# First batch loaded and scaled by halves of its chunks, a weight piece loaded later

## The chip, the cores and the metric

The kernel runs on one core of one Trainium2 chip. The metric is the device time of one execution in microseconds (us). The inputs lie in DRAM, laid out in tiles; every DMA of the kernel is issued by one engine's queue, that of SyncE (SP).

## The reference, cut to what matters

A retention layer (attention with a decay in place of the softmax) is followed by two feed-forward stages. The change touches only how the first layer starts.

```python
# q, k, v: batch 4, heads 8, sequence 576, head size 64
scores = scale * np.matmul(q, k.transpose(0, 1, 3, 2))
ret = scores * Dmat[None]            # Dmat[h, i, j] = gamma[h] ** (i - j) for i >= j, else 0
x = np.matmul(ret, v)                # -> x: 2304 tokens x 512
a, b = x @ moe_w1, x @ moe_w2        # 512 x 1024 each, in float64 weights
x = (a * b @ moe_w3) @ moe_w_out     # then a second stage with moe2_w_in, moe2_alpha, moe2_w_out
```

## The kernel before, in words

The retention of a batch is cut into five chunks of 128 tokens (the last has 64) and into pairs of heads. For a chunk `c`, `scores(c)` multiplies keys by queries on TensorE (PE), VectorE (DVE) multiplies by the mask into `rt`, `moments(c)` makes the sum of key times value that later chunks need, and `values(c)` multiplies the state and `rt` by queries and values; the result is split into `xh` (ScalarE, ACT) and `xl` (DVE). The decay is put into the operands first: `scale` multiplies the queries on GpSimd (POOL), 512 columns (L396) and then 64 (L398) for each pair, and `prep` multiplies the keys on ACT (L389), two instructions of 256 columns for each pair.

Batch 0 is done as two groups, `r0` (pairs 0 and 1) and `r1` (pairs 2 and 3), in a list of steps written out at L602; `s0` and `s1` are their steps. Step `s0[0]` is scores(0) and moments(0), `s0[1]` is scores(1), values(0) and moments(1), and so on. `busy(n)` issues `n` matmuls on zeros (dummies), 26 before the first step and one behind each of the first four steps. `later` holds work for other engines, which `flush()` issues.

The weights of the next product, `w12`, are 16 pieces of 512 KB in float64 (here w0, w1, w2 and so on; `raw` in the trace). `Weights` takes a piece apart in four steps: `_first` is two ACT instructions (L93, L94), `_second` four on DVE (L103 to L108), `_third` one on ACT (L114, the upper part) and `_fourth` one on DVE (L122, the lower part). `tick` issues one such step for each of the four kinds where one is due, last kind first, after `load_until(at[0] + near)` has issued loads; `near` is 4. `tick(n)` begins no piece from number `n` on. `ws.until(n)` ticks until `n` pieces are done.

Behind batch 0 come the product units `ab_unit(0, c)` for c = 0, 1, 2 (L686 to L688), each two products of 12 matmuls (L188) with pieces 2c and 2c+1, with a step of the retention of batch 1 behind each of the two. In `ab_unit` the function `between` (L685) is called behind each product: it ticks the weights, flushes, and then ticks the retention of batch 1, whose first step is `prep` and `scale` of pairs 0 and 1. Before unit c, `ws.until(2c + 2)` stands.

PE, SP and ACT run their instructions in the order in which this program issues them; the order on DVE and POOL is chosen by a planner when the kernel is built.

The queue of SP before the change, in order: decay tables of rows (6 KB), tables of pairs 0 and 1 (448 KB), pairs 0 and 1 of batch 0 (576 KB of queries and keys and 544 KB of keys and values each), w0, tables of pairs 2 and 3, pairs 2 and 3, w1 to w3, pairs 2 and 3 of batch 1 (`load_apart`, 1120 KB each), w4 (by the second tick), pairs 0 and 1 of batch 1 (`loads`), w5 and on.

Of the kernel before, what the change touches and what calls it, by code (L numbers as in the profile page):

```python
# [7 lines left out]
F32 = mybir.dt.float32  # L8
# [3 lines left out]
AF = mybir.ActivationFunctionType  # L12
ALU = mybir.AluOpType
# [133 lines left out]
def retention_moe_kernel(ctx: ExitStack, tc, qk, kv, w_out1, w3t, w12, w_in, w_out2, alpha, c_row, c_pair, out):  # L147
    nc = tc.nc

    def pool(stack, name, bufs=1, **kw):  # L150
        return stack.enter_context(tc.tile_pool(name=name, bufs=bufs, **kw))
# [65 lines left out]
    ws = Weights(nc, raw_room, room, 4)  # L217
# [121 lines left out]
    attn = pool(pa, "attn", side="left")  # L339
# [4 lines left out]
    per_pair = decay.tile([P, NPAIR, 3 * CH + 64], F32, name="per_pair")  # L344
# [4 lines left out]
    kd, gc = per_row[:, 0:H], per_row[:, H:]  # L349
# [13 lines left out]
    def crossed(b):  # L363
        return b >= 2
# [6 lines left out]
    class Retention:  # L371
# [5 lines left out]
            self.ps = slice(pairs[0], pairs[-1] + 1)  # L377
            self.rt, self.state = {}, None

        def prep(self, pairs=None):  # L380
            for p in pairs or self.pairs:
                k = kvt[self.b][p]
                if self.b >= 3:
                    both = k[:, 0:8].rearrange("p (j c) d -> p j (c d)", j=2)
                    nc.gpsimd.tensor_tensor(out=both, in0=both, in1=kd[:, 2 * p:2 * p + 2].unsqueeze(2)
                                            .to_broadcast([P, 2, 4 * D]), op=ALU.mult)
                    continue
                for j in range(2):
                    nc.scalar.activation(k[:, 4 * j:4 * j + 4], k[:, 4 * j:4 * j + 4], AF.Copy,  # L389
                                         scale=kd[:, 2 * p + j:2 * p + j + 1])  # L390

        def scale(self, pairs=None):
            for p in pairs or self.pairs:
                q, by = qt[self.b][p], qs[:, p]
                full = q[:, 0:512].rearrange("p (c i) -> p c i", i=CH)
                nc.gpsimd.tensor_tensor(out=full, in0=full, in1=by.unsqueeze(1).to_broadcast([P, 4, CH]),  # L396
                                        op=ALU.mult)
                nc.gpsimd.tensor_tensor(out=q[:, 512:S], in0=q[:, 512:S], in1=by[:, 0:64], op=ALU.mult)  # L398

        def scores(self, c):  # L400
            b, n = self.b, self.n
# [107 lines left out]
    qt, kt, kvt, vt = ({b: {} for b in range(B)} for _ in range(4))  # L509

    def in_places(b, p, t, src):

        for rows, pp, _ in places(b, p):
            nc.sync.dma_start(out=t[rows], in_=src[pp])  # L514
# [10 lines left out]
    def load_pair(b, p):  # L525
        x = attn.tile([P, 2, S], F32, tag=f"qk{p}", name=f"qk{b}_{p}")
        y = attn.tile([P, 17, D], F32, tag=f"kv{p}", name=f"kv{b}_{p}")
        qt[b][p], kt[b][p], kvt[b][p], vt[b][p] = x[:, 0], x[:, 1], y[:, 0:16], y[:, 16]
        if crossed(b) and p % 2:
            in_places(b, p, x, qk[b, p])  # L530
            nc.sync.dma_start(out=y[:, 0:16], in_=kv[b, p, :, 0:16])
            in_places(b, p, y[:, 16], kv[b, p, :, 16])
        else:
            nc.sync.dma_start(out=x, in_=qk[b, p])
            nc.sync.dma_start(out=y, in_=kv[b, p])

    def load_apart(b, p, n):

        x, y, z = (in_wa(n + m, f"pair{b}_{p}_{m}").bitcast(F32).rearrange("p a b -> p (a b)") for m in range(3))
        qt[b][p], kt[b][p] = x[:, 0:S], y[:, 0:S]  # L540
        vt[b][p] = x[:, S:S + D]
        kvt[b][p] = z.rearrange("p (a d) -> p a d", d=D)
        nc.sync.dma_start(out=qt[b][p], in_=qk[b, p, :, 0])
        nc.sync.dma_start(out=kt[b][p], in_=qk[b, p, :, 1])
        nc.sync.dma_start(out=kvt[b][p], in_=kv[b, p, :, 0:16])
        nc.sync.dma_start(out=vt[b][p], in_=kv[b, p, :, 16])
# [11 lines left out]
    first = ExitStack()  # L558
    psum0 = attention_psum(first, 2)
    nc.sync.dma_start(out=per_row, in_=c_row)  # L560
    nc.sync.dma_start(out=per_pair[:, 0:2], in_=c_pair[:, 0:2])
    load_pair(0, 0)
    load_pair(0, 1)
    ws.load_until(1)
    nc.sync.dma_start(out=per_pair[:, 2:4], in_=c_pair[:, 2:4])
    load_pair(0, 2)
    load_pair(0, 3)
    ws.load_until(4)
    load_apart(1, 2, 10)
    load_apart(1, 3, 13)  # L570
    warm = pool(first, "ps_warm", space=PSUM).tile([P, 512], F32, name="warm")
# [1 line left out]
    def busy(n):  # L573
        for _ in range(n):
            nc.tensor.matmul(warm, idle[:, 0:P], idle[:, :512], start=True, stop=True)

    busy(26)
    r0, r1 = Retention(0, [0, 1], psum0), Retention(0, [2, 3], psum0)
    s0, s1 = r0.steps(), r1.steps()
    r0.scale()  # L580
    r0.prep()

    def keep_busy(step):
        def run():
# [4 lines left out]

    def ready(p):  # L590
        def run():
            r1.scale([p])
            r1.prep([p])
        return run

    def loads():
        load_pair(1, 0)
        load_pair(1, 1)

    one, two, three = ((lambda n=n: ws.tick(n)) for n in (1, 2, 3))  # L600
    b = keep_busy
    for step in (b(s0[0]), b(s0[1]), one, b(s0[2]), one, b(s0[3]), ready(2), one, s0[4], ready(3), one, s1[0],  # L602
                 s0[5], s1[1], loads, two, s1[2], two, s1[3], three, s1[4], three, s1[5]):
        step()
        flush()
# [884 lines left out]
```

## Time and profile before

| | us |
|---|---|
| median of 3 runs | 782.3 |
| lowest, highest run | 779.87, 785.56 |
| the profiled execution | 783.55 |
| its span, from first to last instruction | 781.7 |

The profile is of one execution. PE is busy for 98% of the span, DVE for 75%, ACT for 49%, POOL for 8%. Matmuls are pipelined and their ends are modelled, so the start times of neighbouring matmuls say more than the durations. "Idle before" is the time for which an engine had nothing to run, with what ended it.

### The profile page before, as it was taken

What the parts mean: (1) busy time and instruction counts of PE and PEld (TensorE: products, weight loads), DVE (VectorE), ACT (ScalarE), POOL (GpSimd) and SP (SyncE); (2) the same over time, 40 slices, a digit from 0 to 9 for tenths busy, and PEclk for the clock granted to TensorE, in tenths of its full rate; (3) what the DMA queues carried; (4) which work ended last, traced back from release to release, by engine and by line L of the source; (5) the groups of instructions that cost most, each with busy time, mean ns of one, the idle gap of its engine ahead of it and who ended that gap; (6) DMA issues with size and microseconds to landing.
All of it is one profiled execution on the core that took longest, in us unless ns stands there. A gap on an engine that the chain in (4) does not pass through costs nothing.

```text
span 781.7 us, 13197 instructions
## 1 busy us (share of the span) xinstructions
PE 768.9 (98%) x4928; PEld 688.9 (88%) x4928; DVE 587.3 (75%) x951; ACT 380.4 (49%) x665; POOL 63.8 (8%) x73
## 2 busy tenths in 40 slices
PE   8999999998999999999999999999999999999998
PEld 5788788887788988899999999999999888888887
DVE  4894889569857779688974768778767877777874
ACT  3643474334445466464654546546534444444442
POOL 4410400051000000000000200110200000000000
PEclk9999999999999999999999999999999999999999
DMA  9943965798576667799993796564899754444440
GB/s 353 358 160 105 340 246 202 239 287 259 212 249 204 189 197 256 248 327 368 407 375 138 262 362 225 172 228 154 286 339 366 234 152 128 140 126 136 135 128 28
DMA packets 116225, 182.11 MB, mean 233 GB/s; under 512 B 9920, under 2 KB 82624, under 8 KB 116160
## 3 DMA queue, kind: packets, MB, share of 16 engines
q1 hardware_dynamic: 116160, 181.26, 68.1%
q8 instruction: 39, 0.64, 0.4%
q14 instruction: 26, 0.21, 0.1%
HBM read 117.00 MB, written 64.23 MB: 232 GB/s over the span
## 4 chain that ended last, share of the span: by engine, by line
PE 83%; DVE 7%; DMA 5%; issue 2%; SPq 2%; ACT 1%; POOL 0%; DVEq 0%; ACTq 0%; POOLq 0%
PE h L1063 21%; PE ps L188 19%; PE y L1007 13%; PE o L1208 12%; PE o L1210 6%; PE pw L822 6%; DMA abd<-ab 2%; PE sc L419 2%; PE o L476 2%; DMA cells<-gd 2%; DVE cells L1189 2%; PE o L467 1%; SPq L514 1%; PE st L434 1%; DVE a L108 1%
## 5 line engine op out<-in xcount | busy, mean ns | idle before, releaser
L188 PE MATMUL ps<-xh,w 128*128 128x512 f32 (+1 forms) x640 | 186.1, 372 | 1.8 <-ACT f L651 1.8
L188 PEld LDWEIGHTS ps<-xh,w 128*128 128x128 f32 x640 | 116.1, 188 | 23.3 <-ACT f L651 2.2
L1208 PE MATMUL o<-wop,cells 128*128 128x512 f32 x504 | 126.4, 393 | 0.9 <-DVE cells L1220 0.9
L188 PE MATMUL ps<-xl,w 128*128 128x512 f32 (+1 forms) x320 | 118.0, 369 | 0.0
L1208 PEld LDWEIGHTS o<-wop,cells 128*128 128x128 f32 x504 | 90.8, 189 | 17.7 <-issue 1.4
L1007 PE MATMUL y<-yab,wp 128*128 128x384 f32 x576 | 100.0, 334 | 0.0
L1007 PEld LDWEIGHTS y<-yab,wp 128*128 128x128 f32 x576 | 99.9, 188 | 0.1
L1189 DVE TENSOR_TENSOR cells<-cells,cells 128x1024 fp32r<-128x1024 f32 x63 | 76.4, 1222 | 25.7 <-ACT cells L1183 25.6
L1210 PEld LDWEIGHTS o<-wop,cells 128*128 128x128 f32 x504 | 68.7, 190 | 4.9
L1210 PE MATMUL o<-wop,cells 128*128 128x256 f32 x504 | 70.2, 282 | 0.0
L188 PEld LDWEIGHTS ps<-xl,w 128*128 128x128 f32 x320 | 60.4, 189 | 9.5
L1183 ACT CAST cells<-cells 128x1024 fp32r<-128x1024 f32 x63 | 64.9, 1054 | 7.0 <-DVE cells L1176 4.6
L108 DVE CUSTOM_DVE_ANT_0 a<-a,b 128x1024 uint16<-128x1024 uint16 x72 | 53.2, 738 | 2.9
L1063 PE MATMUL h<-xT,wu 128*128 128x384 f32 x288 | 54.7, 334 | 0.2 <-DVE g L1082 0.2
L1063 PE MATMUL h<-xT,wv 128*128 128x384 f32 x288 | 54.9, 335 | 0.0
L1076 DVE SCALAR_TENSOR_TENSOR g<-h,al,g 128x384 f32<-128x384 f32 x48 | 29.4, 614 | 32.6 <-ACT g L1075 29.5
L637 ACT CAST ab<-f 128x512 fp32r<-128x512 f32 (+1 forms) x40 | 23.1, 577 | 61.2 <-DVE f L641 51.8
L1063 PEld LDWEIGHTS h<-xT,wu 128*128 128x128 f32 x288 | 50.3, 188 | 0.5 <-DVE g L1082 0.5
L1063 PEld LDWEIGHTS h<-xT,wv 128*128 128x128 f32 x288 | 50.3, 188 | 0.3 <-DVE g L1082 0.3
L103 DVE TENSOR_SCALAR a<-a 128x512 f32<-128x512 f32 x72 | 31.9, 443 | 22.9 <-ACT a L93 22.5
L822 PE MATMUL pw<-wo,w 128*128 128x512 f32 x192 | 43.7, 389 | 0.0
L822 PEld LDWEIGHTS pw<-wo,w 128*128 128x128 f32 x192 | 36.0, 188 | 7.4
(130 smaller groups left out, 1139.4 us busy)
## 6 DMA issues: line engine op xcount, KB each, us to landing
gd<-g SPq DMA_DIRECT2D x96, 192.0 KB, 4.4
cells<-gd SPq DMA_DIRECT2D x36, 512.0 KB, 6.3
abd<-ab SPq DMA_DIRECT2D x32, 512.0 KB, 5.2
wod<-wo2u SPq DMA_DIRECT2D x49, 256.0 KB, 4.0
wop<-wod SPq DMA_DIRECT2D x21, 512.0 KB, 6.5
yab<-abd SPq DMA_DIRECT2D x24, 384.0 KB, 8.0
raw<-in_w_dram SPq DMA_DIRECT2D x16, 512.0 KB, 8.0
rawo<-in_w_out_dram SPq DMA_DIRECT2D x16, 512.0 KB, 5.2
```

The source lines that it names most:

```text
L103: nc.vector.tensor_scalar(out=a, in0=a, scalar1=self.LEAST, scalar2=self.MOST, op0=ALU.max, op1=ALU.min)
L108: nc.vector.tensor_tensor(out=a.bitcast(I32), in0=a.bitcast(I32), in1=b, op=ALU.add)
L188: nc.tensor.matmul(ps, a, bb, start=(n == 0), stop=(n == last))
L637: nc.scalar.copy(t[:, 0], f)
L822: nc.tensor.matmul(acc[i], a[:, ic], bb, start=(k == 0 and n == 0), stop=(k == C1 - 1 and n == 2))
L1007: nc.tensor.matmul(ys[o], wpc[c][a][:, oc], yab[b, c][:, bb], start=(c == 0 and i == 0), stop=(c == C1 - 1 and i == 2))
L1063: nc.tensor.matmul(ps, a[:, x, ks], b[:, y, k], start=(fresh and n == 0), stop=(n == 5), skip_group_check=True)
L1076: nc.vector.scalar_tensor_tensor(out=g, in0=ps, scalar=sal[:, c], in1=g, op0=ALU.mult, op1=ALU.max)
L1183: nc.scalar.copy(h.bitcast(F32R), self.q[name])
L1189: nc.vector.tensor_tensor(out=l.bitcast(F32R), in0=q[name], in1=h, op=ALU.subtract)
L1208: nc.tensor.matmul(ps, h[:, k], w[k], start=(fresh and k == 0), stop=(k == C1 - 1), skip_group_check=True)
L1210: nc.tensor.matmul(ps[:, 256:], l[:, k], w[k][:, 0:256], start=False, stop=(k == C1 - 1), skip_group_check=True)
```

## The change

The loads of batch 0 are cut by columns. For a group of two pairs, `load_begin` loads the table of query factors, the first 256 columns of queries and keys, the first two of four chunks of the other keys and values, and then the masks; `load_rest` loads the remaining columns and chunks and the last values. `scale` and `prep` take a range of chunks and are called for each half. Steps `s0[0]` and `s0[1]` give way to `begun` and `second`: scores of chunks 0 and 1 come first, then moments(0), then values(0) and moments(1), with the scaling of the rest between them. `ready(2)` and `ready(3)`, which prepared pair 2 and pair 3, now prepare the first and the second half of both.

The dummies ahead of the first step go from 26 to 10. Two of the pieces that were loaded ahead of batch 1's pairs 2 and 3 (w2 and w3), and w4, which was loaded ahead of its pairs 0 and 1, are now loaded behind all four (`near` is 0 until `loads` sets it to 4). No tick of the list begins w2 any more (`tick(min(n, 2))`).

```diff
-        def prep(self, pairs=None):
+        def prep(self, pairs=None, chunks=slice(0, 4)):
...
                 for j in range(2):
-                    nc.scalar.activation(k[:, 4 * j:4 * j + 4], k[:, 4 * j:4 * j + 4], AF.Copy,
-                                         scale=kd[:, 2 * p + j:2 * p + j + 1])
+                    x = k[:, 4 * j + chunks.start:4 * j + chunks.stop]
+                    nc.scalar.activation(x, x, AF.Copy, scale=kd[:, 2 * p + j:2 * p + j + 1])
...
+                if chunks.stop == 4:
+                    nc.gpsimd.tensor_tensor(out=q[:, 512:S], in0=q[:, 512:S], in1=by[:, 0:64], op=ALU.mult)
...
-    nc.sync.dma_start(out=per_pair[:, 0:2], in_=c_pair[:, 0:2])
-    load_pair(0, 0)
-    load_pair(0, 1)
+    begin, rest = slice(0, 2), slice(2, 4)
...
+    def load_qk(p, cols):
+        nc.sync.dma_start(out=first_x[p][:, :, cols], in_=qk[0, p, :, :, cols])
+
+    def load_kv(p, chunks):
+        y, src = (z[:, 0:16].rearrange("p (g c) d -> p g (c d)", g=4)[:, :, chunks.start * D:chunks.stop * D]
+                  for z in (first_y[p], kv[0, p]))
+        nc.sync.dma_start(out=y, in_=src)
+
+    def load_begin(pairs):
...
+        load_table(pairs, slice(2 * CH + 64, 3 * CH + 64))
+        for p in pairs:
+            load_qk(p, slice(0, 2 * CH))
+        for p in pairs:
+            load_kv(p, begin)
+        load_table(pairs, slice(0, 2 * CH + 64))
+
+    def load_rest(pairs):
+        for p in pairs:
+            load_qk(p, slice(2 * CH, S))
+            load_kv(p, rest)
+            nc.sync.dma_start(out=first_y[p][:, 16], in_=kv[0, p, :, 16])
+
+    load_begin((0, 1))
+    load_rest((0, 1))
     ws.load_until(1)
-    nc.sync.dma_start(out=per_pair[:, 2:4], in_=c_pair[:, 2:4])
-    load_pair(0, 2)
-    load_pair(0, 3)
-    ws.load_until(4)
+    load_begin((2, 3))
+    load_rest((2, 3))
+    ws.load_until(2)
+    ws.near = 0
     load_apart(1, 2, 10)
     load_apart(1, 3, 13)
...
-    busy(26)
+    busy(10)
...
-    r0.scale()
-    r0.prep()
+    for p in r0.pairs:
+        r0.scale([p], begin)
+    for p in r0.pairs:
+        r0.prep([p], begin)
...
-            r1.scale([p])
-            r1.prep([p])
+            if p == 2:
+                r1.scale(None, begin)
+                r1.prep(None, begin)
+            else:
+                r1.scale(None, rest)
+                r1.prep(None, rest)
...
+    def begun():
+        r0.scores(0)
+        r0.scores(1)
+        flush()
+        r0.moments(0)
+        r0.scale(None, rest)
+
+    def second():
+        flush()
+        r0.values(0)
+        r0.moments(1)
+        r0.prep(None, rest)
 
     def loads():
         load_pair(1, 0)
         load_pair(1, 1)
-
-    one, two, three = ((lambda n=n: ws.tick(n)) for n in (1, 2, 3))
+        ws.near = 4
+
+    one, two, three = ((lambda n=n: ws.tick(min(n, 2))) for n in (1, 2, 3))
     b = keep_busy
-    for step in (b(s0[0]), b(s0[1]), one, b(s0[2]), one, b(s0[3]), ready(2), one, s0[4], ready(3), one, s1[0],
+    for step in (b(begun), b(second), one, b(s0[2]), one, b(s0[3]), ready(2), one, s0[4], ready(3), one, s1[0],
                  s0[5], s1[1], loads, two, s1[2], two, s1[3], three, s1[4], three, s1[5]):
```

## Rows read from the trace of the kernel before

**Rows 1.** The page: busy time of each engine, then the chain that ended last.

```profile
PE 768.9 (98%) x4928; PEld 688.9 (88%) x4928; DVE 587.3 (75%) x951; ACT 380.4 (49%) x665; POOL 63.8 (8%) x73
...
PE 83%; DVE 7%; DMA 5%; issue 2%; SPq 2%; ACT 1%; POOL 0%; DVEq 0%; ACTq 0%; POOLq 0%
```

**Rows 2.** Windows by stage: busy time, granted clock, DMA share, GB/s.

```profile
core 0: us, PE busy (x) PEld busy (x) DVE busy (x) ACT busy (x) POOL busy (x), PEclk, DMA share, GB/s
...
30.00:35.00 5.00, 5.00 (x30) 4.12 (x26) 4.28 (x8) 3.44 (x10) 3.36 (x3) 1.00 1.03 422
35.00:40.00 5.00, 4.93 (x44) 3.79 (x44) 4.77 (x7) 4.56 (x10) 1.14 (x2) 1.00 0.48 167
40.00:50.00 10.00, 10.00 (x126) 8.24 (x127) 10.00 (x20) 4.24 (x8) 2.25 (x2) 1.00 0.54 165
...
92.00:96.00 4.00, 2.25 (x10) 1.54 (x10) 1.48 (x3) 1.81 (x4) 1.74 (x2) 1.00 1.03 420
...
100.00:110.00 10.00, 10.00 (x69) 8.13 (x68) 8.55 (x15) 9.21 (x20) 0.00 (x0) 1.00 0.56 221
```

**Rows 3.** Timeline of PE, start to third step: start, length, line, tiles.

```profile
1.45 7.57 PE L575 MATMUL warm<-idle 128*128 128x512 bf16 x26 [1.45 <-DVE idle L167]
8.96 0.49 PE L419 MATMUL sc<-qk 64*128 64x128 f32 x4
10.45 0.49 PE L419 MATMUL sc<-qk 64*128 64x128 f32 x4 [1.00 <-POOL qk L396]
...
13.71 0.71 PE L419 MATMUL sc<-qk 64*128 64x128 f32 x8
```

**Rows 4.** Timeline of POOL and of ACT in the same stretch.

```profile
9.14 1.26 POOL L396 TENSOR_TENSOR qk<-qk,per_pair 128x512 f32<-128x512 f32 x1 [1.15 <-DMA qk<-in_qk_dram]
10.36 0.32 POOL L398 TENSOR_TENSOR qk<-qk,per_pair 128x64 f32<-128x64 f32 x1
...
7.77 0.91 ACT L389 ACTIVATE kv<-kv,per_row 128x256 f32<-128x256 f32 x2 [5.55 <-DMA kv<-in_kv_dram]
10.38 0.91 ACT L389 ACTIVATE kv<-kv,per_row 128x256 f32<-128x256 f32 x2 [1.70 <-DMA kv<-in_kv_dram]
```

**Rows 5.** Timeline of PE, units 0 and 1 and the first idle behind them.

```profile
30.17 0.50 PE L188 MATMUL ps<-xh,w 128*128 128x512 f32 x1
...
36.93 0.93 PE L434 MATMUL st<-kv 128*64 128x64 f32 x7
...
38.08 0.50 PE L188 MATMUL ps<-xh,w 128*128 128x512 f32 x1
...
38.66 0.63 PE L188 MATMUL ps<-xh,w 128*128 128x512 f32 x2
...
43.64 0.50 PE L188 MATMUL ps<-xh,w 128*128 128x512 f32 x1
...
50.21 0.50 PE L188 MATMUL ps<-xh,w 128*128 128x512 f32 x1
...
95.34 0.50 PE L188 MATMUL ps<-xh,w 128*128 128x512 f32 x1 [1.75 <-ACT f L651]
```

**Rows 6.** Timeline of ACT from 28 us: w2, and the order behind the first product.

```profile
28.84 0.69 ACT L93 ACTIVATE a<-raw 128x512 f32<-128x512 f32 x1
...
34.24 0.67 ACT L93 ACTIVATE a<-raw 128x512 f32<-128x512 f32 x1
34.81 0.65 ACT L94 ACTIVATE b<-raw 128x512 int32<-128x512 uint16 x1
35.36 0.57 ACT L651 COPY f<-ps 128x512 f32<-128x512 f32 x1
35.83 1.71 ACT L389 ACTIVATE kv<-kv,per_row 128x256 f32<-128x256 f32 x4
37.44 0.67 ACT L93 ACTIVATE a<-raw 128x512 f32<-128x512 f32 x1
...
39.10 0.62 ACT L637 CAST ab<-f 128x512 fp32r<-128x512 f32 x1 [0.44 <-DVE f L641]
39.63 0.62 ACT L114 CAST w<-a 128x512 fp32r<-128x512 f32 x1
```

**Rows 7.** Timeline of DVE: the lower parts of w3, w4 and w5.

```profile
42.14 0.68 DVE L122 TENSOR_TENSOR w<-a,w 128x512 fp32r<-128x512 f32 x1
...
46.95 0.68 DVE L122 TENSOR_TENSOR w<-a,w 128x512 fp32r<-128x512 f32 x1
...
48.22 0.68 DVE L122 TENSOR_TENSOR w<-a,w 128x512 fp32r<-128x512 f32 x1
```

**Rows 8.** Timeline of SP's queue: pair 3 of batch 0, pair 1 of batch 1.

```profile
6.32 0.33 SPq L534 DMA_DIRECT2D qk<-in_qk_dram  x1
7.70 0.33 SPq L535 DMA_DIRECT2D kv<-in_kv_dram  x1
...
27.02 0.37 SPq L535 DMA_DIRECT2D kv<-in_kv_dram  x1
```

**Rows 9.** The DMA view at those issues: KB, us from issue to landing.

```profile
qk<-in_qk_dram SPq DMA_DIRECT2D x1, 576.0 KB, 10.5
...
kv<-in_kv_dram SPq DMA_DIRECT2D x1, 544.0 KB, 11.7
...
kv<-in_kv_dram SPq DMA_DIRECT2D x1, 544.0 KB, 8.3
```

**Rows 10.** The DMA view and the windows of a stretch of 512-byte packets, 683.5 to 687.

```profile
DMA packets 2272, 1.16 MB, mean 332 GB/s; under 512 B 31, under 2 KB 2271, under 8 KB 2271
...
683.50:687.00 3.50, 3.50 (x21) 3.05 (x20) 2.45 (x2) 2.07 (x3) 0.00 (x0) 1.00 1.13 332
```

**Rows 11.** Windows of the dummies alone, early and late.

```profile
1.40:5.20 3.80, 3.75 (x10) 1.34 (x11) 1.00 0.79 241
5.20:8.96 3.76, 3.76 (x18) 1.55 (x16) 1.00 1.02 416
```

**Rows 12.** The chain that ended last, 60 to 96 us: start, length, what.

```profile
61.98 0.32 SPq L630
...
73.26 1.86 DMA al<-in_alpha_dram
...
85.66 8.45 DMA abd<-ab
```

More of the change, by code (lines that the diff above doesn't have):

```diff
@@ L388, in prep, with scale @@
                 for j in range(2):
-                    nc.scalar.activation(k[:, 4 * j:4 * j + 4], k[:, 4 * j:4 * j + 4], AF.Copy,
-                                         scale=kd[:, 2 * p + j:2 * p + j + 1])
-        def scale(self, pairs=None):
+                    x = k[:, 4 * j + chunks.start:4 * j + chunks.stop]
+                    nc.scalar.activation(x, x, AF.Copy, scale=kd[:, 2 * p + j:2 * p + j + 1])
+        def scale(self, pairs=None, chunks=slice(0, 4)):
             for p in pairs or self.pairs:
                 q, by = qt[self.b][p], qs[:, p]
[L395 to L398, printed above, removed]
+                full = q[:, chunks.start * CH:chunks.stop * CH].rearrange("p (c i) -> p c i", i=CH)
+                nc.gpsimd.tensor_tensor(out=full, in0=full, in1=by.unsqueeze(1)
+                                        .to_broadcast([P, chunks.stop - chunks.start, CH]), op=ALU.mult)
+                if chunks.stop == 4:
+                    nc.gpsimd.tensor_tensor(out=q[:, 512:S], in0=q[:, 512:S], in1=by[:, 0:64], op=ALU.mult)
         def scores(self, c):
@@ L560, in retention_moe_kernel, with load_table @@
     nc.sync.dma_start(out=per_row, in_=c_row)
-    nc.sync.dma_start(out=per_pair[:, 0:2], in_=c_pair[:, 0:2])
-    load_pair(0, 0)
-    load_pair(0, 1)
+    begin, rest = slice(0, 2), slice(2, 4)
+    first_x, first_y = {}, {}
+    def load_table(pairs, cols):
+        ps = slice(pairs[0], pairs[-1] + 1)
+        nc.sync.dma_start(out=per_pair[:, ps, cols], in_=c_pair[:, ps, cols])
+    def load_qk(p, cols):
[6 more added lines that the diff above has]
+        for p in pairs:
+            x = first_x[p] = attn.tile([P, 2, S], F32, tag=f"qk{p}", name=f"qk0_{p}")
+            y = first_y[p] = attn.tile([P, 17, D], F32, tag=f"kv{p}", name=f"kv0_{p}")
+            qt[0][p], kt[0][p], kvt[0][p], vt[0][p] = x[:, 0], x[:, 1], y[:, 0:16], y[:, 16]
+        load_table(pairs, slice(2 * CH + 64, 3 * CH + 64))
[5 more added lines that the diff above has]
+    def load_rest(pairs):
+        for p in pairs:
+            load_qk(p, slice(2 * CH, S))
[3 more added lines that the diff above has]
+    load_rest((0, 1))
     ws.load_until(1)
-    nc.sync.dma_start(out=per_pair[:, 2:4], in_=c_pair[:, 2:4])
-    load_pair(0, 2)
-    load_pair(0, 3)
-    ws.load_until(4)
+    load_begin((2, 3))
+    load_rest((2, 3))
+    ws.load_until(2)
+    ws.near = 0
     load_apart(1, 2, 10)
```

## The prediction

> **What bounds the kernel now.** I read the page first. PE is busy for 98% of the span and carries 83% of the chain that ended last [rows 1], so a change is worth what it takes from PE's waiting or adds to it. The edits end in the first 75 us, so I then read that stretch as PE sees it. PE runs dummies until 8.96, has the scores of pair 0, waits 1.00 us for the scaled queries of pair 1, and goes on at 10.45 [rows 3]. From there it has no idle time worth naming until 93.6 us, where 1.75 us are lost [rows 5]. The last cause, read in the chain, is a run of small loads on SP's queue that begins behind the spill at 61.98, then the load of alpha and a spill that lands late [rows 12]; SP begins that run when PE has finished batch 1, so it moves with PE.
>
> The third view is the DMA. Its share is full and it moves some 420 GB/s until 35 us, and half that behind it [rows 2]. So the start has two bounds, PE's order and one saturated stream of loads, and the reader is to see that what is moved back in the stream lands later by its bytes. The last landing of the stream that matters here is that of the keys and values of batch 1's pair 1: issued at 27.02, landed 8.3 us later, at 35.3 [rows 8, 9]. By the order of the queue 12,422 KB have been loaded by then. Pair 3 of batch 0 landed at 7.70 + 11.7 = 19.4 with 5,894 KB. Between them 6.68 MB took 15.9 us: 420 GB/s.
>
> **The head: a gain on PE of about 2.4 us.** Before the scores of pair 1 could begin, 2,150 KB had to land (tables, pair 0 whole, queries and keys of pair 1: 6 + 448 + 576 + 544 + 576); now it is 646 (6 + 128 + 256 + 256). The difference of 1,504 KB is 3.7 us at 420 GB/s. The queries of pair 1 landed at 9.1 [rows 4], and would land near 5.7, since the shorter runs cost some 0.2 (below). POOL scales 512 columns in 1.26 and 64 in 0.32 us [rows 4], 2.1 ns a column; 256 columns then take 0.72, and pair 1 is scaled by about 6.5 in place of 10.4. The dummies that are left are no bound: the first ten took 3.75 us from 1.45 [rows 3, 11] and end near 5.4. Then the second half decides. scores(2) waits for the remaining columns of pair 1, 2,406 KB into the queue; all of pairs 0 and 1, 2,694 KB, had landed at 10.4 [rows 4]. 288 KB fewer are 0.7 us, the short runs up to there cost 0.95, and POOL's 256 columns 0.72: 11.35, where scores(2) stood at 13.71 [rows 3]. That is the gain of 2.4. The halves of `prep` double ACT's instructions for it (two of 256 columns took 0.91 [rows 4]; bounds for the four: the same 0.91, or 1.8 if each cost what a whole one does), and ACT has idle time for either there. The four dummies behind steps stay. If a half waited for its whole tile, the head would gain nothing; but the scores of pair 1 start at 10.45, when the other POOL instruction on that tile (10.36, 0.32 long) is still running [rows 3, 4], so waits go by regions. Pairs 2 and 3 may give up to 1 us of it back, since their second halves land at the end of a longer stream; by the next parts that changes nothing in the sum.
>
> **The stream: short runs cost 2.3 us.** Batch 0 was read in runs of 2,304 bytes and more, now in 512 (keys and values), 1,024 and 1,280 (queries, keys), 512 and 1,280 (tables), and 256 bytes (last values). A stretch late in the trace with 511 bytes a packet (1.16 MB in 2,272) ran at 332 GB/s with the engines full [rows 10]. From 24.7 ns a packet on each of 16 engines there and 165.8 ns for 4,352 bytes at 420 GB/s, a packet costs an estimated 5.9 ns and its bytes; this gives 377 GB/s for 1,024, 387 for 1,280 and 268 for 256 bytes. Extra time against 420: keys and values (2.10 MB) 1.32, queries and keys 0.28 + 0.27, tables 0.17 + 0.13, last values 0.18. Sum 2.35 us. Bounds: 0 if the run doesn't matter, and 3.5 if all 5.5 MB ran at 332. I take 2.35, since the rate of 332 stands in a row.
>
> **w2 comes last, and ACT waits for it.** Up to and with w2 the queue now holds 12,422 - 1,024 = 11,398 KB (w3 and w4 are behind it). 1,024 KB are 2.5 us, so w2 lands at 35.3 - 2.5 + 2.35 = 35.15; bounds 32.8 and 36.3. Before, w2 was on ACT at 28.84 [rows 6], ahead of the product units at 30.17 [rows 5]. Now the first `between` of unit 0 begins it, and ACT takes its instructions in order: L93 and L94 of w2, then the copy of the first product (L651), `prep` of batch 1's pairs 0 and 1, L93 and L94 of w3, the cast L637, and only then the upper part of w2, L114. Spaced as in the trace [rows 6]: 1.12 + 0.47 + 1.61 + 1.12 + 0.53 + 0.62 = 5.47 us. DVE's lower part takes 0.68 [rows 7] and is wanted by the third matmul of a product, 0.58 us behind the first (38.08 and 38.66 [rows 5]). So unit 1 can start effectively at landing + 5.6: 40.75, with bounds 38.4 and 41.9. Before, it started at 38.08. PE itself would be there at about 35.7 after the gain at the head, and so waits: first for moments(0) of batch 1, whose `prep` ends 3.2 us behind the landing, near 38.35 (before: the last of the four instructions ended near 37.5, inside the group of moments at 36.93 [rows 5, 6]), then for w2. The whole gain is lost there and 2.7 us more (0.3 to 3.8).
>
> What is late next? DVE had w3, w4 and w5 done at 42.8, 47.6 and 48.9 [rows 7]; unit 1's second product stood at 43.64 and unit 2 at 50.21 [rows 5], so w4 had 2.6 us to spare. By the order above w3 has left its first step at landing + 4.3, which leaves it 6.9 us until the second product of unit 1. DVE was full from 40 to 50 [rows 2]; it has w2 more to do there now, about 3 us, but unit 2 is later by 2.7 too, so w4 stays just ahead. So PE is again bound by its own order from there, and the idle time at 93.6 moves along.
>
> **The sum.** Head -2.4, waits for `prep` and w2 +5.1: +2.7 us. The profiled execution took 783.55 (span 781.7 and 1.85 around it), which gives 786.25; it stands 1.25 above the median of its three runs, so for the median 782.3 + 2.7 = 785.0.
>
> **Rivals.**
> - *The stream is sooner, and some gain stays (faster).* Its place is w2's landing. The load ahead of pair 3's last one landed at 6.32 + 10.5 = 16.8, and 544 KB are 1.3 us at 420 GB/s; yet that one came at 19.4 [rows 8, 9]. The stream lost 1.2 us there. If that doesn't recur and short runs cost nothing, w2 lands at 31.6 and unit 1 starts at 37.2, 0.9 us sooner: 781.4. It decides below a landing of 32.5 (38.08 - 5.6). The most it could keep is the head's 2.4: 779.9. For it: the loss is seen once. Against it: both things must be so. Chance 0.25, with the cases between.
> - *Short runs cost nothing, the rest as forecast.* w2 lands at 32.8, unit 1 starts at 38.4: +0.3, 782.6. For it: in the stretch of rows 10 the same engines may have had other limits, such as the layout of the tensor read. Chance 0.17. The Trainium skill ("DMA: Bandwidth & Descriptors", Specifications) puts the least transfer for line rate at 512 bytes, by which this change would pay next to nothing; the row of 511 bytes a packet speaks against it.
> - *PE's clock falls in the new waits (slower).* PE would stand idle for some 2 to 3 us twice between 33 and 41, longer than the 1.75 us at 93.6, around which the granted clock stays at 1.00 (2.4 GHz) [rows 2, 5]. At the start some ten dummies took 3.75 us of PE and some eighteen the next 3.76, though both rows show 1.00 [rows 11]: a stretch at that slower pace costs up to 1.8 us. Then +4.5: 786.8. The ten dummies that are left end about where the pace rose, so the same price could fall at the head, but there the wait for w2 hides it. Chance 0.1.
>
> The forecast keeps 0.48.
>
> **Numbers.** 785.0; its own range is 782.6 to 786.1 (+0.3 to +3.8). The range reaches down to 779.5 (all of the head's gain kept, 779.9) and up to 788.5 (786.8, and half of the 3.3 us by which the highest run stood over the median). A measurement of this kernel can tell about 1%, 7.8 us, from no change; no case reaches that. Faster by over 1% 0.01, slower 0.04 (several waits and a slow clock together), within 0.95.
>
> **What would show it.** Right: PE's scores(2) near 11; ACT's L93 of w2 waiting for `raw` until near 35; PE idle before moments of batch 1 and before unit 1, which starts near 40.8; the same work 2.7 us later behind it. Wrong: w2 landing below 32.5, a DMA rate of 420 in the first 20 us, no wait of ACT on `raw`, or a granted clock under 1.00 in a window between 30 and 50.

## The result, and the profile after

The changed kernel takes 790.76 us (median of 4 runs, 788.42 to 795.53) where the kernel before took 782.22 beside it (4 runs, 779.87 to 785.56): a ratio of 1.0121, interval 1.0088 to 1.0154. It is slower by 8.5 us, 1.2%, and the interval excludes no change; 2.7 were forecast. 790.76 lies above the forecast's own range of 782.6 to 786.1, and above the 788.5 up to which it allowed for its rivals. The profiled execution took 788.42 with a span of 786.6; against the 783.55 of the profile before that is +4.9, and mean granted clocks were 0.991 and 0.997.

The first view is PE's timeline of the changed kernel (start, length, line, tiles, and in brackets the idle time before and what ended it). It answers [rows 3] and [rows 5].

```profile
6.16 0.49 PE L421 MATMUL sc<-qk 64*128 64x128 f32 x4 [0.98 <-POOL qk L397]
...
12.06 1.49 PE L421 MATMUL sc<-qk 64*128 64x128 f32 x8
...
16.54 1.23 PE L421 MATMUL sc<-qk 64*128 64x128 f32 x8
...
31.16 0.50 PE L188 MATMUL ps<-xh,w 128*128 128x512 f32 x1
...
38.32 1.47 PE L436 MATMUL st<-kv 128*64 128x64 f32 x7 [0.29 <-ACT kv L391]
...
42.73 0.80 PE L188 MATMUL ps<-xh,w 128*128 128x512 f32 x1 [2.65 <-ACT w L114]
...
45.30 1.22 PE L188 MATMUL ps<-xh,w 128*128 128x512 f32 x2 [1.35 <-DVE w L122]
...
49.36 0.72 PE L421 MATMUL sc<-qk 64*128 64x128 f32 x8
...
51.94 0.50 PE L188 MATMUL ps<-xh,w 128*128 128x512 f32 x1
...
58.51 0.50 PE L188 MATMUL ps<-xh,w 128*128 128x512 f32 x1
```

The scores begin 2.8 us sooner than before (6.16 against 8.96), scores(2) 1.65 sooner (12.06 against 13.71), and then the gain is gone: scores(3) stands at 16.54, unit 0 at 31.16 where it was at 30.17. Unit 1 starts at 42.73 (38.08 before) and waits again for its third matmul at 45.30 (38.66 before). From its third matmul to the scores behind the product PE takes 4.06 us; in the kernel before it is 2.40, from 38.66 [rows 5] to these scores:

```profile
41.06 0.71 PE L419 MATMUL sc<-qk 64*128 64x128 f32 x8
```

Unit 2 is 8.30 us late, and no wait stands in front of it any more.

Next ACT and DVE of the changed kernel around that wait, the lines that answer to [rows 6] and [rows 7].

```profile
36.17 0.66 ACT L93 ACTIVATE a<-raw 128x512 f32<-128x512 f32 x1 [3.02 <-DMA raw<-in_w_dram]
...
42.06 0.62 ACT L114 CAST w<-a 128x512 fp32r<-128x512 f32 x1 [0.71 <-DVE a L108]
```

```profile
38.08 1.22 DVE L425 TENSOR_TENSOR rt<-sc,per_pair 128x1024 f32<-128x1024 f32 x1 [6.22 <-PE sc L421]
39.22 0.42 DVE L103 TENSOR_SCALAR a<-a 128x512 f32<-128x512 f32 x1
...
41.33 0.69 DVE L108 CUSTOM_DVE_ANT_0 a<-a,b 128x1024 uint16<-128x1024 uint16 x1
...
42.61 0.42 DVE L104 TENSOR_SCALAR a<-a 128x512 uint32<-128x512 uint32 x1
42.94 1.10 DVE L687 TENSOR_TENSOR ab<-f,ab 128x512 fp32r<-128x512 f32 x1
43.97 0.68 DVE L106 SCALAR_TENSOR_TENSOR a<-raw,a 128x512 uint32<-128x512 uint32 x1
44.57 0.68 DVE L122 TENSOR_TENSOR w<-a,w 128x512 fp32r<-128x512 f32 x1
```

w2 is on ACT at 36.17 (35.15 forecast). DVE had been idle for 6.22 us, but its instructions come in a fixed order, and `rt` of batch 1's first scores (those behind unit 0) stands ahead of w2's first step (L103); PE has made those scores only by 38.08. And when the upper part of w2 is done on ACT, DVE does steps of w3 (L104, L106) and the subtraction L687 (the lower part of unit 0's result) before w2's lower part (L122 at 44.57).

Last the windows of the changed kernel (busy us of each engine with its instructions, granted clock, DMA share, GB/s), which answer to [rows 2].

```profile
8.00:10.00 2.00, 1.56 (x9) 0.86 (x9) 0.55 (x1) 1.14 (x4) 0.00 (x0) 1.00 1.09 361
10.00:12.00 2.00, 1.67 (x17) 0.93 (x17) 0.94 (x3) 0.69 (x2) 1.03 (x3) 0.79 1.14 353
12.00:14.00 2.00, 2.00 (x15) 1.53 (x16) 0.62 (x2) 0.95 (x3) 1.60 (x4) 0.50 1.02 364
...
18.00:20.00 2.00, 2.00 (x37) 1.53 (x35) 2.00 (x5) 0.90 (x4) 0.78 (x1) 1.00 1.11 356
...
40.00:42.00 2.00, 0.08 (x2) 0.00 (x0) 1.97 (x5) 1.21 (x3) 0.00 (x0) 0.97 0.08 29
42.00:44.00 2.00, 1.22 (x2) 0.50 (x2) 2.00 (x6) 1.77 (x3) 0.66 (x1) 0.50 0.00 0
...
46.00:48.00 2.00, 2.00 (x6) 1.55 (x5) 1.97 (x5) 1.77 (x3) 0.00 (x0) 0.50 0.91 307
```

The clock is at its lower level, 0.50 (1.2 GHz), twice: at the head, behind a stretch (from 4 us on) in which PE had been busy for only 1.2 to 1.7 us of each 2, and at unit 1, behind PE's idle time from 40.1. PE is busy throughout from 12 to 14 and from 18 to 20, but gets through 15 matmuls from 12 to 14 and 37 from 18 to 20, where the clock is 1.00. The second thing to see is that the DMA moves 353 to 364 GB/s with its share full, where before it moved about 420.

### The profile page after: what moved, and what is told of

Read it like the earlier page. It is cut to its first block, busy times and chain, and to the rows that moved or that the text cites. A ratio compares the mean times of both kernels' runs of the same rounds, so it can differ in the third digit from the quotient of the medians.

```text
span 786.6 us, 13198 instructions
## 1 busy us (share of the span) xinstructions
PE 769.4 (98%) x4912; PEld 689.2 (88%) x4912; DVE 587.0 (75%) x951; ACT 382.0 (49%) x673; POOL 62.3 (8%) x77
## 4 chain that ended last, share of the span: by engine, by line
PE 86%; DVE 6%; DMA 5%; issue 1%; SPq 1%; ACT 1%; DVEq 0%; ACTq 0%
PE ps L188 22%; PE h L1117 22%; PE y L1061 13%; PE o L1262 12%; PE o L1264 6%; PE pw L876 6%; PE sc L421 2%; PE o L478 2%; DMA cells<-gd 2%; PE o L469 1%; DVE cells L1243 1%; DMA abd<-ab 1%; DMA kv<-in_kv_dram 1%; PE st L436 1%; DMA per_pair<-const_pair_dram 1%
## 5 line engine op out<-in xcount | busy, mean ns | idle before, releaser
L108 DVE CUSTOM_DVE_ANT_0 a<-a,b 128x1024 uint16<-128x1024 uint16 x72 | 52.3, 726 | 2.8
L103 DVE TENSOR_SCALAR a<-a 128x512 f32<-128x512 f32 x72 | 32.9, 456 | 23.1 <-ACT a L93 22.6
```

Source lines behind the costliest of these rows:

```text
L103: nc.vector.tensor_scalar(out=a, in0=a, scalar1=self.LEAST, scalar2=self.MOST, op0=ALU.max, op1=ALU.min)
L108: nc.vector.tensor_tensor(out=a.bitcast(I32), in0=a.bitcast(I32), in1=b, op=ALU.add)
```

## The experiments

Times are medians; each ratio is against the kernel before, run on the same chip. A ratio comes from all runs of both kernels, so it differs by up to 0.25% from the quotient of the medians. The last column comes from the list of every run's span and mean granted clock: span x (1 - clock), averaged over the runs. It says how many microseconds of the span the clock was short of 2.4 GHz; it is the clock's full price only where PE had work in that time. For the kernel before, in which PE nearly always has, it is about the right price, as its 66 runs show: the 24 of them with a mean clock of 1.000 have a mean span of 778.6, the 10 with 0.996 and less (mean 0.995) 782.5. By the clock alone, 0.47% of 778.6, they should differ by 3.7; they differ by 3.9.

| kernel | us | ratio [95%] | clock short, us |
|---|---|---|---|
| before (66 runs) | 781 to 782 | | 1.4 |
| after | 790.76 | 1.0121 [1.0088, 1.0154] | 8.3 |
| x1_w2_early | 786.65 | 1.0050 [1.0027, 1.0072] | 4.1 |
| x2_late_only | 785.34 | 1.0046 [1.0025, 1.0067] | 2.5 |
| x3_dummies26 | 790.45 | 1.0102 [1.0067, 1.0138] | 7.5 |
| x4_fill | 790.32 | 1.0094 [1.0066, 1.0122] | 4.5 |
| x9_fill11 | 794.02 | 1.0150 [1.0107, 1.0193] | 5.2 |
| x10_split_short | 787.04 | 1.0071 [1.0044, 1.0098] | 4.6 |
| x11_split_long | 786.88 | 1.0051 [1.0025, 1.0076] | 4.1 |
| x12_split_two | 786.08 | 1.0044 [1.0022, 1.0067] | 4.7 |
| x13_late_chain | 784.20 | 1.0027 [1.0012, 1.0042] | 1.5 |
| x14_after_chain | 787.05 | 1.0084 [1.0054, 1.0115] | 6.4 |
| x8_reordered (11 runs) | 786.17 | 1.0046 [1.0018, 1.0073] | 3.9 |

### The late w2 alone: x2_late_only

The kernel before, with only the loads of w2 to w4 put off:

```diff
-    ws.load_until(4)
+    ws.load_until(2)
+    ws.near = 0
...
+        ws.near = 4
...
-    one, two, three = ((lambda n=n: ws.tick(n)) for n in (1, 2, 3))
+    one, two, three = ((lambda n=n: ws.tick(min(n, 2))) for n in (1, 2, 3))
```

> The kernel before (whole loads, 26 dummies, its steps) with w2 to w4 loaded behind all pairs of batch 1 and w2 not begun in the list. If the late w2 is the cause by itself, w2 lands near 33, unit 1 starts between 38.5 and 40, PE waits 2 us or more for it, and the time is 2 to 7 us over the kernel before, the upper end where the granted clock falls in that wait. If it needs the short runs to be harmful, the time is within 1 us of the kernel before. The landing of w2 against that in the changed kernel (36.2) is the cost of the short runs; expected 2.4 us.

Measured: 785.34, ratio 1.0046, within the 2 to 7 us expected. ACT's first step of w2, then PE at units 1 and 2, in x2:

```profile
32.98 0.66 ACT L93 ACTIVATE a<-raw 128x512 f32<-128x512 f32 x1 [1.03 <-DMA raw<-in_w_dram]
```

```profile
38.52 0.50 PE L188 MATMUL ps<-xh,w 128*128 128x512 f32 x1 [1.11 <-ACT w L114]
...
40.91 1.22 PE L188 MATMUL ps<-xh,w 128*128 128x512 f32 x2 [1.66 <-DVE w L122]
...
47.55 0.50 PE L188 MATMUL ps<-xh,w 128*128 128x512 f32 x1
```

Without the cut loads w2 lands at 32.98; the prediction's bound for that was 32.8, from 420 GB/s. Unit 1 starts 5.54 us later (5.6 forecast). But the third matmul comes 2.39 us behind the first, not 0.58, and the clock falls behind the two waits. Late loading costs 3.9 us by the second product (47.55 against 43.64), and on its own about two fifths of the change's loss (0.46% of 1.21%).

### The cut loads alone: x10_split_short, x12_split_two, x11_split_long

The kernel before, with batch 0's loads cut and nothing else. x10 takes the change's pieces in the old order (24 loads where there were 10, runs of 256 to 1,280 bytes; the tables, not shown, are cut likewise):

```diff
+        elif b == 0:
+            for cols in (slice(0, 256), slice(256, S)):
+                nc.sync.dma_start(out=x[:, :, cols], in_=qk[b, p, :, :, cols])
+            for part in (slice(0, 2 * D), slice(2 * D, 4 * D)):
+                to, src = (z[:, 0:16].rearrange("p (g c) d -> p g (c d)", g=4)[:, :, part] for z in (y, kv[b, p]))
+                nc.sync.dma_start(out=to, in_=src)
+            nc.sync.dma_start(out=y[:, 16], in_=kv[b, p, :, 16])
```

x12 (shown) cuts each load in two with long runs (20 loads, no run under 1,792 bytes, all 128 partitions). x11 (24 loads) does so too, but loads the second half of the keys and values in two parts of 64 partitions:

```diff
+        elif b == 0:
+            for m in range(2):
+                nc.sync.dma_start(out=x[:, m], in_=qk[b, p, :, m])
+            nc.sync.dma_start(out=y[:, 0:8], in_=kv[b, p, :, 0:8])
+            nc.sync.dma_start(out=y[:, 8:17], in_=kv[b, p, :, 8:17])
```

> The kernel before with one edit: the loads of batch 0 and of its tables are cut into the same pieces as in the changed kernel (runs of 256 to 1,280 bytes), one behind the other in the old order; scaling, steps, dummies and the order of the weights stay. If the shorter runs slow the stream, the keys and values of batch 1's pair 1 land near 38.5 in place of 35.3, PE waits for them ahead of unit 1, and the time is 2 to 4.5 us over the kernel before. If only the new order of the steps costs, it is the same as before.

> The kernel before with the loads of batch 0 and of its tables cut into as many DMAs as in the split with short runs, but so that each run keeps 1,792 bytes or more (by query and key, by partitions). If the length of the runs is what slows the stream, pair 1 of batch 1 lands within 0.7 us of 35.3 and the time is that of the kernel before within 1 us. If the number of DMAs or their issue on SP's queue is what slows it, it lands as late as with the short runs, near 38.5.

> The kernel before with each load of batch 0 and of its tables cut in two, all 128 partitions in each and no run under 1,792 bytes (queries apart from keys, the two halves of the keys and values, the tables by pair). The earlier split with long runs also cut by partitions, which could slow it by itself. If the length of the runs is what slows the stream, pair 1 of batch 1 lands within 0.7 us of 35.3 and the time is that of the kernel before within 1.5 us. If the number of DMAs is what slows it, it lands 2 us or more later and the time is 2 to 4 us longer.

Measured: 1.0071, 1.0051 (x11) and 1.0044 (x12). The windows of the first 20 us, in five fences: before, after, x10, x12, and of x11 the second row.

```profile
0.00:8.00 8.00, 6.55 (x22) 2.61 (x23) 0.48 (x1) 1.71 (x3) 1.75 (x6) 1.00 0.73 258
8.00:20.00 12.00, 10.98 (x139) 7.64 (x139) 7.66 (x17) 5.21 (x13) 6.64 (x9) 1.00 1.02 419
```

```profile
0.00:8.00 8.00, 5.16 (x26) 2.28 (x26) 0.48 (x1) 1.73 (x3) 1.61 (x6) 1.00 0.62 176
8.00:20.00 12.00, 11.23 (x104) 7.75 (x106) 7.01 (x15) 5.29 (x16) 5.47 (x10) 0.72 1.10 363
```

```profile
0.00:8.00 8.00, 6.54 (x22) 2.62 (x23) 0.48 (x1) 1.47 (x2) 0.32 (x5) 1.00 0.68 190
8.00:20.00 12.00, 8.78 (x78) 6.36 (x77) 3.85 (x9) 3.31 (x7) 5.46 (x8) 0.72 1.10 368
```

```profile
0.00:8.00 8.00, 6.55 (x23) 2.66 (x24) 0.48 (x1) 1.47 (x2) 0.74 (x5) 1.00 0.70 195
8.00:20.00 12.00, 9.34 (x81) 6.31 (x79) 4.32 (x8) 3.70 (x8) 6.54 (x10) 0.72 1.04 407
```

```profile
8.00:20.00 12.00, 7.98 (x59) 5.37 (x58) 2.79 (x6) 3.32 (x7) 3.96 (x7) 0.76 1.05 308
```

The last two numbers of a row give two separate losses. In the first 8 us the kernels with cut loads move 176 to 195 GB/s (x11 190), with long runs as with short ones, and the kernel before 258: that loss goes with the cutting. From 8 to 20 us x12 is back near 407, and only the short runs stay at 363 to 368: that loss goes with the run length. For x12 they come to 63 x 8 + 12 x 12 = 648 KB, 1.5 us at 420 GB/s; for x10 to 68 x 8 + 51 x 12 = 1,156 KB, 2.8 us; for the changed kernel to 82 x 8 + 56 x 12 = 1,328 KB, 3.2 us. The landings of batch 1's pair 1, the end of the stream, bear the sums out: 35.3 before [rows 8, 9], 36.7 in x12 (issued at 28.13, landed 8.6 later) and 38.35 in x10 (30.75 and 7.6), so 1.4 and 3.05 us late. x12 was expected within 0.7 us if run length alone counted and 2 or more late if the number of loads did: it lies between. x11 is no clean third case: its cut by partitions stays at 308 GB/s from 8 to 20 us with a full share, slower than any other.

What the delay then does is in POOL and PE of x12:

```profile
10.63 1.26 POOL L396 TENSOR_TENSOR qk<-qk,per_pair 128x512 f32<-128x512 f32 x1 [1.62 <-DMA qk<-in_qk_dram]
```

```profile
11.94 0.80 PE L419 MATMUL sc<-qk 64*128 64x128 f32 x4 [2.66 <-POOL qk L396]
```

The queries of pair 1 are scaled at 10.63 (9.14 in [rows 4]), PE waits 2.66 us for them where it waited 1.00 [rows 3], and the clock is 0.50 from 12 to 16 and 0.70 from 16 to 20. Unit 0 starts at 33.55, 3.4 us late. So a stream that is 1.5 us late in the old order costs more than twice that here; the rest goes with the clock, as far as one trace shows it. This profile is of the slowest of x12's ten runs (x10's and x11's are so too); over all its runs x12 is 4.3 us above the kernel before, with 3.3 more in the last column. The trace doesn't show why more loads slow the first 8 us. It isn't that SP issued them too slowly: by 6 us it had issued 2.4 MB in x12, of which 1.0 MB had moved. DMA shares of 0.62 to 0.70 against 0.73 explain a part; the rest is fewer bytes at a full share (x12 moved 271 GB/s at a share of 1.00 from 4 to 6 us, the kernel before 404 at 1.02).

### The change with w2 early: x1_w2_early

The changed kernel with w1 to w3 loaded ahead, as before, and w4 by its tick: `load_until(4)`, no `near`, and `tick(n)` in place of `tick(min(n, 2))`.

> The changed kernel with w1 to w3 loaded ahead of batch 1 again, w4 by the second tick, and w2 begun in the list of steps: the halves and the ten dummies stay. If the late w2 is the cause, ACT has no wait for raw near 33 to 36, PE no wait for the upper part of w2, the granted clock stays at 1.00 between 38 and 50, and the time is within 3 us of the kernel before, some 6 to 8 us under the changed one. If the halves or the dummies are the cause, it stays within 2 us of the changed kernel (790.8).

Measured: 786.65, ratio 1.0050: neither within 3 us of the kernel before, as expected if the late w2 is the cause, nor within 2 of the changed one, as expected if the halves or the dummies are. ACT and PE at unit 1:

```profile
38.75 0.91 ACT L391 ACTIVATE kv<-kv,per_row 128x256 f32<-128x256 f32 x2 [1.54 <-DMA kv<-in_kv_dram]
```

```profile
38.85 0.49 PE L421 MATMUL sc<-qk 64*128 64x128 f32 x4 [1.56 <-POOL qk L397]
...
40.34 0.50 PE L188 MATMUL ps<-xh,w 128*128 128x512 f32 x1
```

The wait for w2 is gone, and another takes its place: batch 1's pair 1 is again last in the stream, and lands at 38.75 where it landed at 35.3 [rows 8, 9]. That is 3.4 us for the cut loads in their new order. Unit 1 starts 2.3 us late, unit 2 4.0. So both halves of the change cost, each about 0.5% alone, and together 1.2%.

### The chain behind w2's landing: x13_late_chain, x14_after_chain

x13 is x2, x14 the changed kernel, each with unit 0's `between` stopped short of w3, so that w3's steps don't stand ahead of w2's:

```diff
-    between = cycle(r, 7 / 6, 1, 6, True)
...
+        between = cycle(r, 7 / 6, 1, 6 if c else 3, True)
```

> The kernel with only the late w2 (whole loads, 26 dummies), with one more edit: behind unit 0's products no tick begins w3, so that w2's steps stand ahead of w3's on ACT and DVE. w2 still lands near 33. If the time was lost in the order of the work behind the landing, unit 1's third matmul has its lower part near 38 to 39 in place of 40.9, the granted clock stays at 1.00 from 40 to 46, unit 1's second product starts near 44 to 45 in place of 47.6, and the time is within 1.5 us of the kernel before. If the landing itself costs, the time stays some 3.6 us over it.

> The changed kernel with the same edit: behind unit 0's products no tick begins w3. w2 lands near 36.2 as before. If the order of the work behind the landing made the price larger than the sum of the prediction, unit 1's third matmul comes near 41 to 42 in place of 45.3, its second product near 47 in place of 51.9, and the time is 2 to 5 us under the changed kernel (790.8), which leaves it 2 to 5 us over the kernel before. If not, it stays within 1.5 us of it.

PE of x13, then of x14:

```profile
38.29 0.50 PE L188 MATMUL ps<-xh,w 128*128 128x512 f32 x1 [0.40 <-ACT w L114]
...
40.31 0.73 PE L188 MATMUL ps<-xh,w 128*128 128x512 f32 x2 [1.28 <-DVE w L122]
...
45.38 0.50 PE L188 MATMUL ps<-xh,w 128*128 128x512 f32 x1
```

```profile
43.34 0.50 PE L188 MATMUL ps<-xh,w 128*128 128x512 f32 x1 [2.28 <-ACT w L114]
...
44.23 1.22 PE L188 MATMUL ps<-xh,w 128*128 128x512 f32 x2 [0.15 <-DVE w L122]
```

The windows from 40 to 44 us, x2 and then x13:

```profile
40.00:44.00 4.00, 3.09 (x7) 2.48 (x8) 3.86 (x8) 1.24 (x3) 0.00 (x0) 0.61 0.31 69
```

```profile
40.00:44.00 4.00, 3.69 (x28) 2.88 (x30) 4.00 (x9) 0.62 (x2) 0.73 (x1) 1.00 0.11 15
```

In x13 w2 lands at 32.78, as in x2, and the third matmul at 40.31 is 0.6 sooner; but PE's waits are 0.40 and 1.28 instead of 1.11 and 1.66, the clock stays at 1.00, and from the third matmul to the second product PE takes 5.07 us where x2 takes 6.64. That is 1.6 us of clock behind waits that differ by 1.1. In x14 the order of DVE gives 2 us: the third matmul stands 7.07 us behind w2's landing (37.16), not 9.13. The clock still falls, behind a wait of 2.28. Against what was expected, x13's third matmul is late (40.31, not 38 to 39) and its time is 2.4 us over the kernel before, not within 1.5; x14, whose w2 landed 1 us later than expected (third matmul at 44.23, not 41 to 42), is 3.7 us under the changed kernel, within the 2 to 5 expected. Ratios fall from 1.0046 to 1.0027 and from 1.0121 to 1.0084; the intervals overlap, so for the size I go by the traces, one of each kernel.

### Dummies and fillers: x3_dummies26, x4_fill, x9_fill11

x3 is the changed kernel with `busy(26)` for `busy(10)`. x4 and x9 put idle work ahead of unit 1's products, six and eleven of these:

```diff
+        if c == 1:
+            t = pm.tile([P, 512], F32, tag="pm", name="fill")
+            for _ in range(6):
+                nc.tensor.matmul(t[:, 0:256], per_pair[:, 0, 0:128], per_pair[:, 0, 0:256], start=True, stop=True)
```

> The changed kernel with 26 dummies ahead of the first step in place of 10. scores(2) still waits for the second halves near 12. If the dummies kept the clock, the granted clock is 1.00 from 10 to 18 and the steps of pairs 0 and 1 are some 2 to 3 us sooner by 18; if the late w2 decides, unit 1 still starts near 42.7 and the time stays within 1.5 us of the changed kernel. If the fall of the clock at the head is what costs, the time is 3 us or more under it.

> The changed kernel with six matmuls of the masks (128 x 256, float32, some 2.6 us together) between moments(0) of batch 1 and unit 1, in the time in which PE waited for w2. They compute nothing that is used. If the fall of the clock behind that wait is part of the price, the granted clock stays at 1.00 from 40 to 50, unit 1's first product takes about 3 us from its third matmul in place of 4.1, its second product starts 1.5 to 3.5 us sooner than 51.9, and the time falls by as much. If only the wait itself costs, the time is the same or up to 2.6 us longer.

> As the fill of six, with eleven matmuls of the masks (some 4.7 us) between moments(0) of batch 1 and unit 1, so that they also cover the wait of the third matmul for the lower part of w2, behind which the granted clock fell in the last kernel. They compute nothing that is used. If the fall of the clock has a price of its own, the granted clock stays at 1.00 from 40 to 50, unit 1's second product starts near 50.3 in place of 51.9, and the time is 1 to 2 us under the changed kernel. If not, the second product stays near 52.

x3 gives 1.0102, no difference from the change. With 26 dummies PE is all but full to 15.0 and the clock 1.00, but then it stands still and the clock falls all the same (0.58 from 17 to 21). PE of x3:

```profile
16.98 0.46 PE L436 MATMUL st<-kv 128*64 128x64 f32 x8 [2.00 <-issue]
```

x4 fills the wait for the upper part of w2 (unit 1 starts at 42.89) and holds the clock at 1.00 to 44, but the wait for the lower part lies behind the fill. PE of x4:

```profile
45.47 1.22 PE L188 MATMUL ps<-xh,w 128*128 128x512 f32 x2 [1.84 <-DVE w L122]
```

The clock is 0.52 from 46 to 49 after it: nothing won. In the last column x4's runs are 3.8 us better than the changed kernel's, and the medians differ by 0.4, so that column is no price here. In x9's profile PE waited 2.36 us for `prep` ahead of the fillers, the clock fell there, and the fillers themselves ran at 0.50 and held unit 1 up to 49.78. So x9 doesn't answer what it was for, the clock's price at unit 1; it shows that fillers cost when they come late. But its head does say something. Windows, then PE of x9:

```profile
8.00:20.00 12.00, 10.80 (x130) 8.28 (x130) 7.43 (x16) 5.94 (x17) 5.11 (x10) 1.00 1.08 359
```

```profile
30.95 0.50 PE L188 MATMUL ps<-xh,w 128*128 128x512 f32 x1
```

Its head is that of the changed kernel, with ten dummies, and here the clock doesn't fall; yet unit 0 starts at 30.95, no sooner than before (30.17). PE has waited for DVE on the way, 0.81, 0.36 and 0.56 us from 26 to 30.4. So the gain of the head is lost without any fall of the clock.

### A gentler version: x8_reordered, x15_reordered_again

The kernel before with whole loads in a new order (queries and keys of both pairs ahead of keys and values), scores of two chunks first, 22 dummies, and only w4 put off (cut here):

```diff
+        for p in pairs:
...
+            nc.sync.dma_start(out=x[p], in_=qk[0, p])
+        nc.sync.dma_start(out=per_pair[:, ps, 0:2 * CH + 64], in_=c_pair[:, ps, 0:2 * CH + 64])
+        for p in pairs:
+            nc.sync.dma_start(out=y[p], in_=kv[0, p])
...
+    def begun():
+        r0.scores(0)
+        r0.scores(1)
+        flush()
+        r0.values(0)
```

> A version made from the kernel before that keeps long runs: the query factors and the whole queries and keys of two pairs are loaded ahead of their masks, keys and values; scores of chunks 0 and 1 and values(0) stand ahead of the moments; 22 dummies; of the pieces only w4 is moved behind batch 1's pairs, w2 stays where it was. scores(2) should start near 12.3 (before: 13.71) and unit 1 0.5 to 1.3 us sooner than 38.08, for a time 0.5 to 1.5 us under the kernel before. If PE is held by the pairs of batch 1 or by DVE behind the head, unit 1 starts at 38.08 and the time is the same.

> The reordered version with long runs once more, for a profile, since the last one was of a disturbed execution. scores(2) near 12.3; unit 1 later than 38.08 by some 2 to 4 us, since its time was 0.5% over the kernel before: the trace should show what holds PE there (the pairs of batch 1, w3, or a fall of the granted clock).

Measured: 786.17 (median of 11 runs; a twelfth, the profiled one, took 1600.69), ratio 1.0046, where 0.5 to 1.5 us under the kernel before were expected. x15 is a profile of the same kernel, of a run of 789.34. There scores(2) start at 14.39, not at the 12.3 expected. The DMA moves 411 to 419 GB/s from 8 to 20 us there, but PE is busy for only 2.55 of the 4 us from 8 to 12, and the clock is 0.92, 0.50 and 0.73 in the three windows of 4 us from 8 to 20; unit 0 starts at 31.98. No version tried here beats the kernel before.

## Why the prediction was wrong

**The sum failed; the order of events held.** As forecast, w2 lands last, ACT takes its first step (L93) when it lands and `prep` of batch 1 behind it, PE waits for w2, and behind unit 1 PE's own order decides again. (The wait for moments is 0.29 us, since PE comes there later than forecast.) Three terms were too small, one of which, PE's clock, the sum had at nothing; and the sign that the prediction named against itself, a granted clock under 1.00 between 30 and 50, came. For the third matmul of unit 1, which decides, and unit 2, the profiled pair gives this:

| step | forecast | measured | difference |
|---|---|---|---|
| w2 lands | 35.15 | 36.17 | 1.02 |
| landing to unit 1's first matmul | 5.6 | 6.56 | 0.96 |
| first to third matmul | 0.58 | 2.57 | 1.99 |
| third matmul to next scores | 2.40 | 4.06 | 1.66 |

The differences add up to 5.63; with the 2.67 forecast (40.75 - 38.08) that is the 8.30 by which unit 2 is late.

**The chain behind the landing (2.95 of the 5.63).** The step that failed is the one that took the spacing of ACT from [rows 6] and DVE's 0.68 from [rows 7] and put them one behind the other. It counted w2's own instructions, but not what stands ahead of them on DVE. DVE waits for batch 1's first scores (L425) before w2's L103, which moves L108 and with it L114 back by 1 us; and w3's steps and L687 stand between w2's L108 and L122, 2 us more. x14, which takes w3 out of there, gets 2.06 of it back. In x3, where DVE takes three of w2's steps ahead of these scores, the third matmul stands 8.02 us behind the landing (35.98 and 44.00).

**PE's clock.** It was a rival with a chance of 0.1, at up to 1.8 us a fall. The price per fall was about right (1.66 at unit 1, 1.6 between x2 and x13); the chance was too small, and the 0.48 for no fall too large. The argument against it was the 1.75 us of idle time at 93.6 around which the clock stays at 1.00. But the trace of the kernel before has a second idle time, which the prediction doesn't use: its rows of PE end at 110 us. PE and the windows there:

```profile
182.70 1.65 PE L419 MATMUL sc<-qk 64*128 64x128 f32 x12 [2.38 <-DVE rt L423]
```

```profile
180.00:184.00 4.00, 1.62 (x14) 1.30 (x14) 4.00 (x8) 2.57 (x5) 0.54 (x1) 0.83 1.02 399
184.00:188.00 4.00, 4.00 (x45) 3.53 (x44) 4.00 (x8) 1.51 (x3) 1.66 (x1) 0.75 0.70 273
```

Around 2.38 us of idle time the clock falls (0.58 in the window from 182 to 186): a row that speaks for this rival was in the trace all along, and the forecast waits of "some 2 to 3 us" lay nearer to it than to the 1.75. It doesn't decide by itself, though: in the profile after, the same place has an idle time of 2.22 us with a clock of 1.00, and x2 lost it behind 1.11 and 1.66. There was also more than one fall: over the runs the clock is short by 8.3 us, and by 1.4 before. Of the 9.6 us between the mean spans (789.6 and 780.0) that is 6.9, if all of it told. It doesn't: in the profiled run 3.4 us of it fall at the head (10 to 18 us), and unit 0 starts at 31.16, hardly later than in x9 (30.95), which has no fall there; at unit 1 it is another 3.4 (40 to 50 us), of which 1.66 tell, since PE was idle in much of that time.

**The stream.** 3.2 us (36.17 against x2's 32.98), where 2.35 were forecast with a bound of 3.5. Sum and place were nearly right, the reason only half: by x10 and x12 about 1.5 us come with cutting the loads, which the prediction priced at nothing, and what short runs add to that is 1.2 (x10, which has four more loads than x12) to 1.6 us (the changed kernel, whose order of loads differs too). The rate of 332 GB/s from [rows 10] was a fair guide for run length. The rival that short runs cost nothing falls: x10, most of it in runs of 512 to 1,280, moves 368 GB/s from 8 to 20 us, and x12 with long runs 407. The Trainium skill ("DMA: Bandwidth & Descriptors", Specifications) puts the least transfer for line rate at 512 bytes. x10's rate beside x12's speaks against that.

**The head.** scores(2) at 12.06, 0.7 later than forecast: a gain of 1.65 instead of 2.4. POOL had the rest of pair 1's queries only at 11.97, since the stream was slower than forecast from its start (176 GB/s over the first 8 us, 258 before). By unit 0 the gain has turned into a loss of 1.0 (31.16 against 30.17), where the prediction let pairs 2 and 3 take back "up to 1 us" and said that this changes nothing. It isn't quite nothing: the scores for which DVE waits ahead of w2's L103 come from this late PE, so a part of the 0.96 us in the table hangs on it; how much, no run here separates. The rival that some gain stays falls as well: no run with w2 put off has it on ACT before 32.78.

**The dummies.** No bound, as forecast; x3 shows no difference in time. Its clock falls too, if later, with 26 of them, and x9's, with ten, doesn't fall at the head: the number of dummies alone doesn't decide it.

**Why the median is farther off than the profile.** Between 58 and the end the profiled pair comes closer, from 8.3 to 4.9 us: idle time ahead of a product is 0.81 at 102.69 where it was 1.75 [rows 5], and the fall at 182 doesn't occur. This is one pair of executions. The profile before lies 1.25 above its median, the profile after is the fastest of four, and the 4 runs after go with their clock: spans of 786.6 and 788.4 at 0.991 and 0.993, 789.5 at 0.989, 793.7 at 0.985. What decides from run to run where the clock falls behind 60 us stays open.

## What to carry to other kernels

When work is put off until its last moment, follow every engine that touches it in its own order, and count what is queued ahead of each step there; the durations of the steps alone gave 6.2 us for a chain of 9.1. Read the whole trace for waits of the size that a change would make, and look at the granted clock behind each: here waits of 2 to 3 us on PE cost 1.6 to 1.7 more after they had ended. And a load that is cut to bring its first part sooner costs time in the stream, here 1.5 us for the number of loads and about as much for the short runs: ask what stands behind it in the same queue, and whether that is on the path, as w2 and batch 1 were here.

## What was not expected of the hardware

- Cutting ten loads into twenty at the start, with runs of 1,792 bytes and more, took the mean rate of the first 8 us from 258 to 195 GB/s, and the scores of pair 1 began 1.5 us later (11.94 against 10.45). Why is open.
- A stream with some loads of 64 partitions in place of 128 (x11) moved 308 GB/s from 8 to 20 us at a share of 1.05, where whole loads moved 419 at 1.02.
- The spread of the runs of the kernel before goes with the granted clock: mean spans of 778.6 us at 1.000 and 782.5 at 0.995.
